# Loading later head pairs one stage earlier, holding one pair's loads for VectorE, and a changed order of stages, in windowed attention followed by a gated FFN

## The chip, the cores and the metric

The kernel runs on 1 core of one Trainium2 chip. The metric is the device time in microseconds (us); smaller is better. The trace's own span is some 1.8 us shorter than that time, so spans are compared with spans and times with times. Ratios are of fast runs alone; medians and ranges are of all runs of a kernel, a few slow ones among them. One trace, named below, is of a slow run and is not compared. The record also has the mean granted TensorE clock of every run: 0.998 or more, or 0.994 or less, and nothing between. Traces at 1.000 show no stretch of half clock, those from 0.981 to 0.994 one or two.

## The reference, cut to what matters

```python
# batch 4, 8 heads, 768 positions, head size 64; 4 sink positions, window of 128
scores = scale * q @ k^T;  keep = is_sink | (0 <= row - col < 128)
a = softmax(where(keep, scores, -1e9));  attn = a @ v           # (4, 8, 768, 64)
x = attn, heads side by side: (3072, 512)
out = (relu(x @ w_gate) * (x @ w_val)) @ w_out                  # d_ff = 1536
```

## The kernel before

Two heads make a pair; pairs are numbered 0 to 15, four to a batch. A pair's attention is cut into stages: three score groups (`s(0..2)`), the second half of the pair before it (`v`), preparing the next pair and loading later ones (`t`), and the first half of its own normalization (`v0`). A plan weaves these stages between the chunks of the FFN, which keeps TensorE filled. All engines follow one program order; waits come from data and buffers.

```python
def unit_stages(x):
    u, prev, nxt = U[x], at(x - 1), at(x + 1)
    def s(gi):
        def f():
            ...                                   # (cut)
            if gi == 0 and nxt is not None and nxt.xbar:   # pairs 8 to 15
                nxt.X()                           # DMA transposes of keys, queries (SyncE)
            u.S(gi)                               # scores, exponential, mask
        return f
    def v():  ...  norm(prev, 1)                  # (cut)
    def t():
        if nxt is not None:
            if not nxt.xbar:
                nxt.T(not on_array)               # pairs 1 to 7: transposes on TensorE
            nxt.sinkk()                           # VectorE: sink keys, needs nxt's kT
        if x == 3:   load(6)
        elif x == 4: load(7)
        elif x >= 5: held(x + 3)
        if 4 <= x < 6:
            for c in ((0,), (1, 2))[x - 4]: load_wo(c)
        if at(x + 3) is not None:
            casts(at(x + 3), "kqv")               # GpSimd: float32 to bf16
            ...                                   # (cut)
        if x in (0, 1, 3, 4): load_w((0, 1, 1, 2, 3)[x])
        if x == 0:   load(5)
    ...

def held(x):                                      # the loads wait for VectorE
    if x < len(U):
        nc.vector.memset(U[x].stg[0:1, 0:1], 0.0)
        load(x)

PLAN = ((0, 28), (24, 50), (48, 62), (71, 74))    # (chunk, stages done by then)
```

`load` puts keys, queries and two value halves of a pair (1.18 MB) in SyncE's DMA queue. `load_w` and `load_wo` put weights in GpSimd's. A staging buffer serves every fourth pair.

The softmax here doesn't subtract the row's maximum and nothing guards it: scores larger than these inputs give would overflow.

Of the kernel before, what the change touches and what calls it, by code (L numbers as in the profile page):

```python
# [33 lines left out]
def kernel(  # L34
# [179 lines left out]
    def warm(n):  # L214

        if not warm_ps:
            warm_ps.append(ps_gv.tile([128, 512], F32, name="warm", tag="gv"))
        for _ in range(n):
            nc.tensor.matmul(out=warm_ps[0][:, 0:128], lhsT=ident[:], rhs=ident[:], start=True, stop=True,
                             skip_group_check=True)  # L220

    def load_w(c):
        n = d_ff // 4
        for w, dst in ((moe_w_gate, wg), (moe_w_val, wv)):
            nc.gpsimd.dma_start(out=dst[:, :, c * n:(c + 1) * n],  # L225
                                in_=w.rearrange("(ko ki) n -> ki ko n", ki=128)[:, :, c * n:(c + 1) * n])

    def load_wo(c):
        nc.gpsimd.dma_start(out=wo[:, 4 * c:4 * c + 4, :],
                            in_=moe_w_out.rearrange("(ko ki) n -> ki ko n", ki=128)[:, 4 * c:4 * c + 4, :])  # L230


    def setup_pool():
        make_identity(nc, ident)
        t0, a = bias[:, 0:255], bias[:, 503:754]
        for x, w, d in ((t0, 255, 0), (a, 251, 4)):
            nc.gpsimd.memset(x, 0.0)
            nc.gpsimd.affine_select(out=x, in_=x, compare_op=Alu.is_ge, fill=NEG, base=d,
                                    pattern=[[1, w]], channel_multiplier=-1)
            nc.gpsimd.affine_select(out=x, in_=x, compare_op=Alu.is_ge, fill=NEG, base=127 - d,  # L240
                                    pattern=[[-1, w]], channel_multiplier=1)

    def setup_slot(s):
        nc.vector.memset(kT[s][:, S:872], 0.0)

    def setup_m0():

        cp, ms = nc.gpsimd.tensor_copy, nc.gpsimd.memset
        ms(bias[0:4, 0:128], 0.0)
        ms(bias[0:4, 128:255], NEG)  # L250
        cp(bias[:, 255:503], bias[:, 503:751])
        ms(bias[0:4, 255:503], 0.0)
        ms(bias[0:4, 503:627], NEG)
# [64 lines left out]
    with tc.manual_schedule():  # L318
        U = [Unit(i) for i in range(B * NP)]
        on_array = []  # L320

        def at(x):
            return U[x] if 0 <= x < len(U) else None

        def casts(u, what, eng=nc.gpsimd):
            for w in what:
                u.cast(w, eng)

        def load_t(b):

            nc.sync.dma_start(out=vt[b % 2][:], in_=v[b, :, 744:768, :].rearrange("h s d -> s h d"))  # L331

        def cast_t(b):
            nc.gpsimd.tensor_copy(v6[b % 2][0:24, :, :], vt[b % 2][:])

        def load(x):
            if not U[x].p:
                load_t(U[x].b)
            for f in (lambda e: U[x].load_kq("k", e), lambda e: U[x].load_kq("q", e),
                      lambda e: U[x].load_v(e, 0), lambda e: U[x].load_v(e, 1)):  # L340
                f(nc.sync)

        def held(x):
# [5 lines that stand above are left out]
        for y in ("k0", "q0", "k1", "q1", "v1", "t", "k2", "q2", "v2", "k3", "q3", "v3"):  # L349
            if y == "t":  # L350
                load_t(0)
            elif y[0] in "kq":
                U[int(y[1])].load_kq(y[0], nc.sync)
            else:
                for h in (0, 1) if y[0] == "v" else ("ab".index(y[0]),):
                    U[int(y[1])].load_v(nc.sync, h)
        nc.vector.memset(ones[:], 1.0)
        setup_pool()
        setup_m0()
        nc.scalar.activation(ee[0][:, 0, 0, 0:64], ones[:], Act.Exp, bias=0.0, scale=1.0)  # L360
        for h in range(2):
            U[0].load_v(nc.scalar, h)
        for x in range(2):
            nc.vector.memset(v6[x][:], 0.0)
        setup_slot(0)
        setup_slot(1)
        warm(36)
        casts(U[0], "k", nc.vector)
        casts(U[0], "q", nc.scalar)
        casts(U[1], "kq")  # L370
        casts(U[0], "v")
        cast_t(0)
        casts(U[1], "v")
        casts(U[2], "kqv")
        load(4)


        stages = []
# [6 lines that stand above are left out]
                    if gi == 0 and u.p == 0:  # L385
                        xTs[u.b] = xpool.tile([128, NP, S], BF16, name="xT")
                    if gi == 0 and nxt is not None and nxt.xbar:
                        nxt.X()
                    u.S(gi)
                    if x == 0 and gi < 2:  # L390
                        warm(5)
                return f

            def v():
                if prev is not None:
                    norm(prev, 1, ps_at if on_array else ps_gv)
# [4 lines that stand above are left out]
                        nxt.T(not on_array)  # L401
                    nxt.sinkk()
                if x == 3:
                    load(6)
                elif x == 4:
                    load(7)
                elif x >= 5:
                    held(x + 3)
                if 4 <= x < 6:
                    for c in ((0,), (1, 2))[x - 4]:  # L410
                        load_wo(c)
                if at(x + 3) is not None:
                    casts(at(x + 3), "kqv")
                    if (x + 3) % NP == 0:
                        cast_t((x + 3) // NP)
                if x in (0, 1, 3, 4):
                    load_w((0, 1, 1, 2, 3)[x])
                if x == 0:
                    load(5)
            def v0():  # L420
                norm(u, 0, ps_at if on_array else ps_gv)

            def both(f, g):
                return lambda: (f(), g())
            if x < NP:
                return [s(0), v, s(1), t, s(2), v0]
            return [both(v, s(0)), both(t, s(1)), both(v0, s(2))] if x >= 8 else [s(0), v, s(1), t, s(2), v0]

        def first():
            U[0].T(True)  # L430
            U[0].sinkk()
            setup_m1()
        stages.append(first)
        for x in range(len(U)):
            stages += unit_stages(x)
        stages.append(lambda: norm(U[-1], 1))

        si = 0
        f2 = deque()
        total = len(stages)  # L440

        ORDER = [(0, h, m) for g in range(0, FM, 3) for h in range(2) for m in range(g, g + 3)]
        ORDER += [(b, h, m) for b in range(1, B) for h in range(2) for m in range(FM)]
        PLAN = ((0, 28), (24, 50), (48, 62), (71, 74))

        def want(ci):
            for (c0, w0), (c1, w1) in zip(PLAN, PLAN[1:]):
                if ci <= c1:
                    return w0 + (w1 - w0) * (ci - c0) // (c1 - c0)
            return total  # L450
        count = {}
        n = S // 2
        for ci, (b, h, m) in enumerate(ORDER):
            if b not in hTs:
                hTs[b] = hpool.tile([128, FM, S], BF16, name="hT", tag="hT")
            while si < min(total, want(ci)):
                stages[si]()
                si += 1
            if not ci:
                on_array.append(1)  # L460
            chunk(b, h * n, n, m)
            for _ in range(min(3, len(f2))):
                f2.popleft()()
            count[b, h] = count.get((b, h), 0) + 1
            if count[b, h] == FM:
                for t in range(3 * h, 3 * h + 3):
                    w = d_model // 2 if (b, t) == (B - 1, 5) else d_model
                    for c in range(0, d_model, w):
                        for mm in range(FM):
                            f2.append(lambda b=b, t=t, mm=mm, c=c, w=w: ffn2(b, t, mm, b == B - 1, c, w))  # L470
        while f2:
            f2.popleft()()
# [33 lines left out]
```

## Time and profile before

| | |
|---|---|
| time, median of the first 3 runs | 260.46 us (259.57 to 260.71) |
| span of the profiled run | 258.7 us, TensorE busy 249.4 us |
| TensorE's waits in the middle of the run | 2.0 us for `hT` at 74 us, 1.1 us for `wv` at 30 us |
| granted TensorE clock | 1.00 |

In the lines of waits, the columns are who waited, the source line, for whom, the us in total, the number of waits and the longest. In the timelines they are start, duration, engine, line, operation and tiles; the bracket gives the idle time just before and what ended it. `kT<-kn` is a DMA transpose of keys; `stg` are staging buffers.

### The profile page before, as it was taken

The numbers are of one execution on the slowest core, as the hardware profiler recorded it, in microseconds if no ns is written. First come the engines' busy times: TensorE is split into PE (matmuls) and PEld (weight loads), VectorE is DVE, ScalarE is ACT, GpSimd is POOL, SyncE is SP. The second block draws the span as 40 slices with busy tenths as digits, with TensorE's granted clock in tenths as the row PEclk, the third lists the DMA queues.
The fourth block names the chain that finished last, engine by engine and source line by source line (L and its number), as shares of the span: only waits on it lengthen the run. The fifth ranks groups of instructions, "written<-read, shape, count | busy, mean of one in ns | idle before, by whom it ended". The sixth has DMA issues, their size and how long they took to land.

```text
span 258.7 us, 5201 instructions
## 1 busy us (share of the span) xinstructions
PE 249.4 (96%) x2046; PEld 143.5 (55%) x2046; DVE 144.5 (56%) x313; ACT 115.6 (45%) x188; POOL 62.3 (24%) x94
## 2 busy tenths in 40 slices
PE   7999799999969999999999999999999999999994
PEld 7565466565545555546555555556555555555443
DVE  2598869886748564756656665756664322322100
ACT  3887665647424444443535344344533332333212
POOL 6779538801535221404040210000000000000000
PEclk9999999999999999999999999999999999999999
DMA  7999999999989948869491961311011101111132
GB/s 213 309 279 253 246 257 197 196 198 199 218 125 239 197 111 157 129 145 138 85 242 43 184 104 42 61 43 41 3 41 41 42 1 41 43 41 41 41 112 94
DMA packets 77320, 33.56 MB, mean 130 GB/s; under 512 B 64368, under 2 KB 74352, under 8 KB 77296
## 3 DMA queue, kind: packets, MB, share of 16 engines
q1 hardware_dynamic: 69920, 28.12, 48.5%
q0 software_dynamic: 5808, 4.72, 12.1%
q10 hardware_dynamic: 1568, 0.39, 0.7%
q8 instruction: 16, 0.26, 0.5%
q14 instruction: 8, 0.07, 0.1%
HBM read 28.51 MB, written 6.29 MB: 135 GB/s over the span
## 4 chain that ended last, share of the span: by engine, by line
PE 68%; DMA 13%; SPq 8%; POOL 6%; issue 2%; DVE 1%; ACT 0%; POOLq 0%; DVEq 0%; ACTq 0%
PE op L310 23%; PE gp L290 19%; PE vp L296 18%; DMA stg<-in_v_dram 11%; PE ops L206 5%; SPq L119 4%; PE sps L181 3%; SPq L114 2%; DMA kT<-kn 2%; POOL vn L129 2%; SPq L111 1%; SPq L331 1%; POOL kn L126 1%; POOL vn L130 1%; POOL wg L225 1%
## 5 line engine op out<-in xcount | busy, mean ns | idle before, releaser
L298 DVE TENSOR_TENSOR hT<-gs,vp 128x384 bf16<-128x384 f32 x96 | 52.8, 550 | 54.4 <-PE vp L296 52.7
L290 PE MATMUL gp<-xT,wg 128*128 128x384 bf16 x384 | 78.5, 327 | 2.0 <-DVE hT L298 2.0
L296 PE MATMUL vp<-xT,wv 128*128 128x384 bf16 x384 | 78.1, 326 | 1.1 <-DMA wv<-in_moe_w_val_dram 1.1
L293 ACT ACTIVATE gs<-gp 128x384 f32<-128x384 f32 x96 | 47.1, 490 | 61.5 <-PE gp L290 60.3
L310 PE MATMUL op<-wo,hT 128*128 128x512 bf16 (+1 forms) x300 | 74.4, 370 | 0.0
L185 ACT ACTIVATE ee<-sps 128x1006 bf16<-128x1006 f32 (+2 forms) x48 | 46.1, 966 | 46.9 <-PE sps L181 46.8
L296 PEld LDWEIGHTS <-wv 128*128 128x128 bf16 x384 | 37.5, 98 | 26.2 <-DMA wv<-in_moe_w_val_dram 1.5
L290 PEld LDWEIGHTS <-wg 128*128 128x128 bf16 x384 | 34.0, 98 | 31.8 <-issue 6.7
L310 PEld LDWEIGHTS <-hT 128*128 128x128 bf16 x300 | 29.4, 98 | 25.0
L187 DVE TENSOR_TENSOR ee<-ee,msk 128x1006 bf16<-128x1006 bf16 (+2 forms) x36 | 25.1, 698 | 11.3 <-ACT ee L185 11.3
L126 POOL CAST kn<-stg 128x768 bf16<-128x768 f32 x15 | 13.2, 879 | 59.0 <-DMA stg<-in_k_dram 39.6
L314 ACT COPY ot<-op 128x512 f32<-128x512 f32 (+1 forms) x25 | 14.2, 569 | 24.5 <-PE op L310 24.5
L275 DVE STREAM_TRANSPOSE R<-ops 128x384 f32<-128x384 f32 x24 | 13.9, 581 | 12.6 <-PE ops L206 12.5
L278 DVE STREAM_TRANSPOSE R<-rc 128x384 f32<-128x384 f32 x32 | 18.5, 578 | 1.1
L280 DVE TENSOR_TENSOR xT<-ops,R 128x384 bf16<-128x384 f32 x32 | 17.8, 557 | 1.7
L206 PEld LDWEIGHTS <-ones 128*64 128x64 bf16 x288 | 12.3, 109 | 11.2 <-issue 10.8
L129 POOL CAST vn<-stg 128x768 bf16<-128x768 f32 x16 | 13.3, 832 | 15.0 <-DMA stg<-in_v_dram 15.0
L126 POOL CAST qn<-stg 128x768 bf16<-128x768 f32 x15 | 13.3, 888 | 11.9 <-DMA stg<-in_q_dram 7.1
L206 PE MATMUL ops<-ee,vn 128*64 128x255 bf16 (+7 forms) x256 | 15.3, 240 | 0.2 <-DVE xT L280 0.2
L181 PE MATMUL sps<-qT,kT 64*128 64x251 bf16 (+2 forms) x128 | 14.7, 252 | 0.5 <-ACT qT L154 0.4
L181 PEld LDWEIGHTS <-kT 64*128 64x128 bf16 x128 | 6.3, 93 | 12.9 <-issue 10.5
L181 PE MATMUL sps<-qT,kTs 64*128 64x248 bf16 (+1 forms) x96 | 12.3, 253 | 0.0
(57 smaller groups left out, 135.5 us busy)
## 6 DMA issues: line engine op xcount, KB each, us to landing
stg<-in_k_dram SPq DMA_DIRECT2D x16, 384.0 KB, 4.9
stg<-in_q_dram SPq DMA_DIRECT2D x16, 384.0 KB, 5.4
out_dram<-ot SPq DMA_DIRECT2D x23, 256.0 KB, 2.0
stg<-in_v_dram SPq DMA_DIRECT2D x30, 192.0 KB, 5.4
wg<-in_moe_w_gate_dram POOLq DMA_DIRECT2D x4, 384.0 KB, 7.7
wv<-in_moe_w_val_dram POOLq DMA_DIRECT2D x4, 384.0 KB, 9.8
wo<-in_moe_w_out_dram POOLq DMA_DIRECT2D x3, 512.0 KB, 13.6
stg<-in_v_dram ACTq DMA_DIRECT2D x2, 192.0 KB, 6.4
```

The costliest lines, as they stand in the source:

```text
L126: cp((self.kn if what == "k" else self.qn)[:], self.staging(what).rearrange("p h (n d) -> p n h d", d=64))
L129: eng.tensor_copy(self.vn[:], self.staging("v"))
L181: nc.tensor.matmul(out=ps[:, h, c:c + w], lhsT=self.kw(j, r), rhs=qT[s][r, qa:qa + w], start=not self.biased, stop=True, skip_group_check= ...
L185: nc.scalar.activation(x, ps[:, :, 0:c], Act.Exp, bias=0.0, scale=scale)
L187: nc.vector.tensor_tensor(x, x, bc(msk[:, m0:m0 + c], 2), op=Alu.mult)
L206: nc.tensor.matmul(out=ps[1 - what][64 * h:64 * h + 64, qa - q0:qa - q0 + w], lhsT=self.vw(j, h) if what else ones[:], rhs=ee[s][:, gi, h, ...
L278: nc.vector.transpose(r[:, 1, 0:w], bass.AP(a.tensor, a.offset, [a.ap[0], [1, nb], [0, 32]]))
L290: nc.tensor.matmul(out=gp[:, 0:n], lhsT=wg[:, ko, m * 128:(m + 1) * 128], rhs=x[:, ko, c0:c0 + n], start=ko == 0, stop=ko == KO - 1)
L293: nc.scalar.activation(gs[:, 0:n], gp[:, 0:n], Act.Relu, bias=0.0, scale=1.0)
L296: nc.tensor.matmul(out=vp[:, 0:n], lhsT=wv[:, ko, m * 128:(m + 1) * 128], rhs=x[:, ko, c0:c0 + n], start=ko == 0, stop=ko == KO - 1)
L298: nc.vector.tensor_tensor(hT[:, m, c0:c0 + n], gs[:, 0:n], vp[:, 0:n], op=Alu.mult)
L310: nc.tensor.matmul(out=op, lhsT=hTs[b][:, m, t * 128:(t + 1) * 128], rhs=wo[:, m, c0:c0 + n], start=m == 0, stop=m == FM - 1)
```

## The change

The intent is to give the first weights the DMA engines to themselves (pair 5, which stood beside them, now waits for VectorE), to load pairs 8 to 15 one stage earlier, and to let scores run ahead of the previous pair's normalization.

```diff
                 if x == 3:
+                    held(5)
+                    casts(U[5], "kqv")
                     load(6)
                 elif x == 4:
                     load(7)
-                elif x >= 5:
-                    held(x + 3)
+                if x >= 4:
+                    held(x + 4)
 ...
-                if at(x + 3) is not None:
+                if at(x + 3) is not None and x != 2:
+                    pass
                     casts(at(x + 3), "kqv")
 ...
-                if x == 0:
-                    load(5)
 ...
             if x < NP:
-                return [s(0), v, s(1), t, s(2), v0]
+                return [s(0), s(1), v, t, s(2), v0]
 ...
-        PLAN = ((0, 28), (24, 50), (48, 62), (71, 74))
+        PLAN = ((0, 28), (6, 32), (24, 50), (48, 62), (71, 74))
```

## The prediction

> **What bounds the kernel now.** I name a pair of heads by its index 0 to 15 (batch 0 is pairs 0 to 3); the title's "sixth pair" is pair 5. I read the page's busy times first, then who TensorE waited for, then the chain of waits, then the timelines of SyncE, GpSimd and VectorE around each wait, then the DMA queues stretch by stretch. First the page (busy us, share, instructions):
>
> ```profile
> PE 249.4 (96%) x2046; PEld 143.5 (55%) x2046; DVE 144.5 (56%) x313; ACT 115.6 (45%) x188; POOL 62.3 (24%) x94
> ```
>
> Then TensorE's own waits (who waited for whom: us in total, times, longest):
>
> ```profile
> PE gp L290 <- DVE hT L298: 2.0, 1, 2.0
> ...
> PE vp L296 <- DMA wv<-in_moe_w_val_dram: 1.1, 1, 1.1
> ...
> PE sps L181 <- ACT qT L154: 0.4, 1, 0.4
> ```
>
> TensorE is the bound: 249.4 of 258.7 us. The other 9.3 us are 2.0 us at the start, 3.3 us at the tail (240 us on: busy 15.4 of 18.7), and three waits that an order of loads could touch: 1.1 us for the first value weights at 30 us, 0.4 us at 27 us, and 2.0 us near 74 us. Everything the change could win is therefore 3.5 us, or 1.3%. What it could lose is not limited so.
>
> The 2.0 us wait says "hT", but the VectorE timeline names its cause: VectorE sat 4.93 us at pair 8's sink keys, which come by a DMA transpose. Next, lines of the timelines of SyncE, VectorE and TensorE that lead there (start, duration, in brackets the idle time before):
>
> ```profile
> 47.18 0.37 SPq L111 DMA_DIRECT2D stg<-in_k_dram  x1
> ...
> 51.01 12.26 SPq L119 DMA_DIRECT2D stg<-in_v_dram  x2
> 63.35 2.67 SPq L111 DMA_DIRECT2D stg<-in_k_dram  x1
> ...
> 69.84 1.62 SPq L135 DMA_TRANSPOSE kT<-kn  x1
> ...
> 74.87 0.41 DVE L161 COPY kTs<-kT 128x372 bf16<-128x372 bf16 x1 [4.93 <-DMA kT<-kn]
> ...
> 75.87 0.81 PE L290 MATMUL gp<-xT,wg 128*128 128x384 bf16 x4 [1.97 <-DVE hT L298]
> ```
>
> Pair 8's loads are issued from 47.18, pair 9's from 63.35, and only then pair 8's transposes at 69.84. SyncE's queue is in program order, so pair 8's transposes stand behind pair 9's bytes; the last value cast of pair 9 starts at 74.31, when its data has landed, and the transpose lands at 74.84. TensorE resumes 1.0 us later, at 75.87, and from there to the end has no wait worth naming. So **the time is 75.87 us plus 182.8 us**, and it moves one for one with that landing as long as TensorE is there waiting for it.
>
> The DMA queues between 53 and 63.5 us show why pair 8 needs 20 us from issue to landing:
>
> ```profile
> q0 software_dynamic: 1804, 1.57, 91.1%
> q1 hardware_dynamic: 1788, 0.45, 32.7%
> ```
>
> Equal numbers of packets go from the weight queue (q0) and from SyncE's (q1), but a weight packet carries 768 bytes or more, a row of pair 8 only 256. So q1 gets a quarter of the bytes, 0.043 MB/us, and the sum is 0.19 MB/us. From 45.5 to 66 us the same view gives 3.00 + 1.09 MB, 0.20 MB/us with all DMA engines busy.
>
> **What the Trainium skill says.** "DMA: Bandwidth & Descriptors", section "Queues, rings and completion order": each DMA engine takes turns between its queues packet by packet, and consumes one queue's descriptors in ring order. The trace agrees with both: 1804 against 1788 packets, and the transpose landing just behind pair 9. The same page's section "Issuing engines are not separate DMA queues": transfers from different issuers share the same 16 engines. Holding pair 5 back thus does give the weights its bandwidth, but only moves the bytes. "TensorE: Matmul & The Clock Gate", opening table, calls VectorE's queue a strict FIFO; the 4.93 us in which VectorE did none of the ready FFN products agrees.
>
> **The change part by part.**
>
> (a) Scores of the second group before the previous pair's normalization, pairs 0 to 3. The same instructions move; nothing is added. TensorE is busy 9.75 of 10 us between 10 and 20 us and 9.4 in the next 10, so all there is to win is the 0.4 us for `qT` at 27 us: ScalarE's idle gaps of 0.7 to 0.8 us before the second exponential go and its copies end earlier. Against it, two score banks must be released sooner. I give it 0.3 us.
>
> (b) Pair 5 waits for VectorE. Its loads, issued from 19.39 before, now follow a 59 ns memset of VectorE behind pair 4's sink keys. Those end at 27.0 now; with (a) I put it at 26.5, so the loads are issued from 26.6. The first weights (issued 21.25, landing about 28 and 31 now) should land near 28 both, as pair 4's bytes are nearly through by 22 us: the wait of 1.1 us goes. But the second weights are issued at 26.3 and pair 5 now meets those instead. Keys and queries are 0.79 MB (2 x 384 KB). In 30 to 36 us q1 shared with weights and moved 0.94 MB, 0.157 MB/us: 5.0 us. From 26.6, with about 1.4 us to the first byte (76.7 for an issue at 75.40), they land near 33 to 34.5; the query cast takes 0.83 us and the transposes on TensorE 0.33 us after it. TensorE arrives for these transposes at about 31.8 (33.03 before less the 1.1 us), has them at 35 to 36.5 against an end of 33.70 before. **The wait of 1.1 us is exchanged for one of 3 to 4 us**; net 1.3 to 2.8 us later at this point.
>
> (c) Pairs 8 on are loaded one stage earlier (the held load of pair x+4, not x+3, at stage t of pair x). This reads as a gain: pair 8 is released near 38 us, not 47. But the transposes of pair 8 stay where they were, at the first stage of pair 7, and stage t of pair 6 comes before that. Before, that stage issued pair 9; now it issues pair 10. So **pair 8's transposes now stand behind pair 10 too**: 1.18 MB more (k, q, two v). The windows 67 to 72 us show 1.17 MB of such rows in 5.0 us, so 5.0 us. What comes off: between 42.5 and 45 us the engines moved only 59 GB/s (pair 7 done, third weights not started), about 0.35 MB below the 0.20 MB/us that they do later. Pair 8 is now queued there and fills a part. But pair 5, held, makes pairs 6 and 7 end about 1 us later, so I count 0.25 MB, 1.2 us. Sum: the transposes land 3.8 us later, at about 78.7 rather than 74.84. What was a stall of 4.9 us for VectorE becomes one of 6 to 8.
>
> (d) The new plan point (6, 32) runs 4 stages in the first 6 chunks where 5.5 ran, and returns to the old plan at chunk 24. Nothing is added; stage t of pair 4 stays at chunk 2 and that of pair 7 at chunk 21. I count 0.
>
> The sum: (a) and (b) leave TensorE 1 to 2.8 us late on the way to 74 us, but there it stood waiting for 2.0 us and now the target is 3.8 us later, so these are absorbed. What remains is (c): 260.46 + 3.8 = **264.3 us**, 1.5% longer.
>
> **Rivals.**
>
> First: the earlier loads free the transpose (the evident intent). If pair 8's transposes land by 73 us, the 2.0 us go, and with (b) at its cheapest the time is about 259.5 us. For it: pair 8 can be released 9 us earlier. Against it: the DMA engines are full from 46 to 72 us in the page's row, so an earlier release only joins the same line, and SyncE's program order puts pair 10 ahead of the transposes. I see no way to over 2% faster: it needs 5.2 us and all waits that the change touches are 3.5.
>
> Second: TensorE's wait in (b) decides instead. If pair 5 is starved by the weights as pair 8 was (3.7 us passed between its issue at 47.18 and its bytes), its queries land at 37 and the shift at chunk 2 is 4 to 5 us. Then the end is again 263.5 to 265 us. Both lie on the same path, so the later one counts, not the sum.
>
> Third: the bytes in front of the transposes cost more. At 0.19 MB/us (the rate next to weights) pair 10 costs 6.2 us, with no credit for the gap: 266.7 us, over the 2% line at 265.7.
>
> **Range and chances.** From rival one at its best, with a little lost, to rival three and a little: 261.3 to 267.3 us. Faster by over 2%: 0.01. Slower by over 2% needs the transposes 5.2 us later, which is between my estimate and rival three: 0.24. Within 2%: 0.75.
>
> **What will show it.** (b): TensorE waits for GpSimd's cast of `qn` or `kn` at 32 to 36 us, and the wait for `wv` is gone. (c): in SyncE's timeline the loads of three pairs stand between 40 us and the first transpose, and VectorE waits 6 us or more for `kT<-kn`, to land at 77 to 80. The wait of TensorE for `hT` near 74 to 80 us is then 2 to 5 us. After it nothing differs: the rest takes 182.8 us, within 1 us. I am wrong if that transpose lands before 74.8, if it is issued before pair 10's loads, or if a new wait appears after 80 us because later transposes, too, stand behind one pair more.

## The result, and the profile after

The changed kernel takes 268.38 us (median of 4 runs, 266.89 to 268.88); the kernel before, run beside it, 260.58 us (259.57 to 261.67). The ratio is 1.0289, 95% interval 1.0229 to 1.0349: slower, and above the predicted range of 261.3 to 267.3. A ratio is the mean time of one kernel's fast runs over that of the other's of the same rounds, so it is not quite the ratio of the medians.

Busy time and TensorE's clock by slice, from the page of the changed kernel:

```profile
PE 252.4 (95%) x2023; PEld 145.0 (54%) x2046; DVE 143.9 (54%) x314; ACT 116.1 (44%) x188; POOL 61.3 (23%) x94
...
PEclk9999967999997999999999999999999999999999
```

The clock row is new: all nines before, and now two dips, in slices 6 and 7 (33 to 47 us) and in slice 13 (80 to 87 us). The matmuls are the same (23 of their records are missing from the later trace), and TensorE is busy 3.0 us longer. TensorE's waits in the changed kernel:

```profile
PE tkq L149 <- POOL kn L126: 2.7, 1, 2.7
PE gp L290 <- DVE hT L298: 2.4, 1, 2.4
PE tkq L149 <- POOL qn L126: 1.6, 1, 1.6
```

The wait of 1.1 us for `wv` is gone, and 4.3 us for pair 5's casts stand in its place. The wait for `hT` is still there, 7 us later. Lines of the timelines that lead to it:

```profile
71.38 0.53 SPq L111 DMA_DIRECT2D stg<-in_k_dram  x1
...
76.42 1.62 SPq L135 DMA_TRANSPOSE kT<-kn  x1
...
81.72 0.41 DVE L161 COPY kTs<-kT 128x372 bf16<-128x372 bf16 x1 [5.23 <-DMA kT<-kn]
...
82.73 0.81 PE L290 MATMUL gp<-xT,wg 128*128 128x384 bf16 x4 [2.40 <-DVE hT L298]
```

The load at 71.38 is pair 10's; pair 8's transposes come after it. TensorE resumes at 82.73, against 75.87 before: 6.9 us of the 8.3 us by which the span grew. From there to the end it takes 184.3 us against 182.8, the other 1.4 us. Two stretches, with columns stretch, length, busy time of TensorE, its weight loads, VectorE, ScalarE and GpSimd, granted clock, DMA share and GB/s, show what that is:

```profile
37.00:42.00 5.00, 4.94 (x24) 2.55 (x25) 1.01 (x5) 2.76 (x4) 2.01 (x4) 0.50 1.02 281
...
84.00:86.00 2.00, 2.00 (x11) 0.68 (x11) 1.90 (x5) 0.06 (x1) 0.05 (x1) 0.50 1.29 261
```

After each of the two waits TensorE's granted clock is 0.50 for some us. The first FFN product after pair 5's transposes, a group of four matmuls, in the changed kernel and in the kernel before:

```profile
37.67 1.49 PE L290 MATMUL gp<-xT,wg 128*128 128x384 bf16 x4
```

```profile
33.70 0.81 PE L290 MATMUL gp<-xT,wg 128*128 128x384 bf16 x4
```

TensorE is busy, and it goes at half pace: the next group starts 1.28 us later here (38.95), 0.65 us later there (34.35).

### The profile page after: what moved, and what is told of

Its sections match the earlier page's. It is cut to its first block, busy times and chain, and to the rows that moved or that the text cites. A ratio compares the mean times of both kernels' runs of the same rounds, so it can differ in the third digit from the quotient of the medians.

```text
span 267.0 us, 5185 instructions
## 1 busy us (share of the span) xinstructions
PE 252.4 (95%) x2023; PEld 145.0 (54%) x2046; DVE 143.9 (54%) x314; ACT 116.1 (44%) x188; POOL 61.3 (23%) x94
## 4 chain that ended last, share of the span: by engine, by line
PE 82%; DMA 7%; DVE 6%; issue 1%; ACT 1%; POOL 1%; SPq 0%; DVEq 0%; ACTq 0%; POOLq 0%
PE gp L290 25%; PE op L310 23%; PE vp L296 23%; PE ops L206 7%; DMA stg<-in_q_dram 5%; PE sps L181 4%; DMA kT<-kn 2%; DVE R L278 1%; DVE R L275 1%; DVE kTs L161 1%; DVE xT L280 1%; PE tkq L149 1%; DVE rc L276 1%; ACT ee L185 0%; PE sps L176 0%
## 5 line engine op out<-in xcount | busy, mean ns | idle before, releaser
L290 PE MATMUL gp<-xT,wg 128*128 128x384 bf16 x384 | 79.8, 331 | 2.9 <-DVE hT L298 2.4
L296 PE MATMUL vp<-xT,wv 128*128 128x384 bf16 x384 | 79.4, 330 | 0.4 <-DVE R L275 0.3
L310 PE MATMUL op<-wo,hT 128*128 128x512 bf16 (+1 forms) x277 | 71.3, 373 | 1.2
L129 POOL CAST vn<-stg 128x768 bf16<-128x768 f32 x16 | 14.0, 873 | 31.3 <-DMA stg<-in_v_dram 15.6
L126 POOL CAST qn<-stg 128x768 bf16<-128x768 f32 x15 | 12.4, 830 | 12.1 <-DMA stg<-in_q_dram 7.4
L161 DVE COPY kTs<-kT 128x372 bf16<-128x372 bf16 x16 | 6.6, 415 | 15.9 <-ACT kT L154 10.6
```

The costliest lines, as they stand in the source:

```text
L126: cp((self.kn if what == "k" else self.qn)[:], self.staging(what).rearrange("p h (n d) -> p n h d", d=64))
L290: nc.tensor.matmul(out=gp[:, 0:n], lhsT=wg[:, ko, m * 128:(m + 1) * 128], rhs=x[:, ko, c0:c0 + n], start=ko == 0, stop=ko == KO - 1)
L296: nc.tensor.matmul(out=vp[:, 0:n], lhsT=wv[:, ko, m * 128:(m + 1) * 128], rhs=x[:, ko, c0:c0 + n], start=ko == 0, stop=ko == KO - 1)
L310: nc.tensor.matmul(out=op, lhsT=hTs[b][:, m, t * 128:(t + 1) * 128], rhs=wo[:, m, c0:c0 + n], start=m == 0, stop=m == FM - 1)
```

## The experiments

The theory after the result: two waits on one path. Pair 5's hold makes TensorE late (its wait, then half clock). Pair 10's place ahead of pair 8's transposes makes those land late. The later of the two at about 80 us sets the end, and half clock comes on top. Rivals: the order of stages costs; the hold is all of it; the place of the transposes is all of it; the clock is no cost of its own.

### The order alone (e1_order)

```diff
-                return [s(0), v, s(1), t, s(2), v0]
+                return [s(0), s(1), v, t, s(2), v0]
-        PLAN = ((0, 28), (24, 50), ...
+        PLAN = ((0, 28), (6, 32), (24, 50), ...
```

> The kernel before with only the two changes of order: second score group ahead of the previous normalization for pairs 0 to 3, and the new plan point. Theory (the loss lies in the two changes of loads): within 0.8 us of before, 259.7 to 261.3; TensorE's 0.4 us wait for qT near 27 us gone, the wait near 74 us again about 2 us. Rival (the order itself costs): over 263 us.

Measured: 261.12 us against 260.48, ratio 1.0032 (1.0007 to 1.0057). Who TensorE waited for:

```profile
PE sps L181 <- DVE kTs L162: 1.6, 4, 0.6
...
PE gp L290 <- DVE hT L298: 1.0, 1, 1.0
```

The wait for `qT` went as foretold; the wait near 74 us is 1.0 us where about 2 was expected. Four short waits for the sink keys, 1.6 us in all, came between 13 and 29 us: the reordered scores ask for them sooner. They don't set the end of the traced run: TensorE still waits for pair 8's keys afterwards and resumes at 76.09, against 75.87. What the 0.3% is made of is not shown; 12 of these 20 runs had a stretch of half clock (mean clock 0.994 or less), 8 of the 23 of the kernel before. So the order wins nothing, and it is not the loss.

### The hold of pair 5 alone (e2_hold5)

```diff
                 if x == 3:
+                    held(5)
+                    casts(U[5], "kqv")
                     load(6)
-                if at(x + 3) is not None:
+                if at(x + 3) is not None and x != 2:
-                if x == 0:
-                    load(5)
```

> The kernel before with only pair 5's loads held for VectorE (and its casts moved). Theory: two effects on one path. TensorE waits about 4.3 us for the casts of pair 5 and runs at half clock for some us after, and the 1.1 us wait for wv goes: TensorE is 5 to 6.5 us late at 74 us. Pair 8's transpose, with only pair 9 ahead of it, lands about 2 to 3 us later than the 74.84 of before, so TensorE waits for it hardly any more. Time 264 to 265.5 us. If the transposes alone set the time (rival), it is 262 to 263.5.

Measured: 264.32 us, ratio 1.0156 (1.0093 to 1.0219), inside the theory's range and outside the rival's. TensorE's waits, then VectorE's arrival at the transposed keys of pair 8:

```profile
PE tkq L149 <- POOL kn L126: 2.3, 1, 2.3
PE tkq L149 <- POOL qn L126: 1.8, 1, 1.8
```

```profile
75.92 0.43 DVE L161 COPY kTs<-kT 128x372 bf16<-128x372 bf16 x1 [0.31 <-DMA kT<-kn]
```

TensorE lost 4.1 us here, the granted clock was 0.72 on average from 37 to 43 us, and the keys landed near 75.9, 1 us later than before (the expectation had 2 to 3). VectorE waited only 0.3 us for them and TensorE not at all: with the hold alone, TensorE's lateness is the loss.

### The earlier loads alone (e3_early)

```diff
-                elif x >= 5:
-                    held(x + 3)
+                if x >= 4:
+                    held(x + 4)
```

> The kernel before with only the held loads one stage earlier (pair x+4 at stage t of pair x), so that pair 10 stands ahead of pair 8's transposes. Theory: no wait near 32 us beyond the 1.1 us for wv; the transpose lands 3.5 to 5.5 us later than 74.84, at 78.3 to 80.3; TensorE waits 5.5 to 7.5 us there and then runs some us at half clock, 1 to 2 us more. Time 265 to 267.5 us. Rival (the earlier loads are harmless, the held pair 5 is all of the loss): 258.5 to 261.

Measured: 267.2 us, ratio 1.0255 (1.0204 to 1.0307). The lines where VectorE and TensorE go on:

```profile
79.11 0.37 DVE L161 COPY kTs<-kT 128x372 bf16<-128x372 bf16 x1 [6.49 <-DMA kT<-kn]
```

```profile
80.07 1.44 PE L290 MATMUL gp<-xT,wg 128*128 128x384 bf16 x4 [3.47 <-DVE hT L298]
```

The keys land at 79.1 us, 4.2 us later than before, in the fastest of the four runs (266.04 us); TensorE waits 3.5 us where the expectation had 5.5 to 7.5. In this run it had itself come later: it waited 1.9 us for `wv`, ran at 0.66 clock from 32 to 37 us, and took 1.46 us for a group of four matmuls that took 0.81. From 80 to 84 the clock was 0.60 on average. The verdict does not rest on that: the loads, meant as a help, cost 6.7 us by themselves.

### The changed kernel with the transposes first (e4_xfirst)

```diff
-                if x >= 4:
+                if 4 <= x < 6:
                     held(x + 4)
 ...
                     if gi == 0 and nxt is not None and nxt.xbar:
                         nxt.X()
+                        held(x + 3)
```

> The changed kernel, but from pair 10 on the held loads are issued just behind the transposes of the stage, not ahead of them, so that only pair 9 stands ahead of pair 8's transposes. Theory: the transpose lands 5 us earlier than in the changed kernel, at 76 to 77.5; TensorE arrives there at 80 us (late from pair 5's wait and half clock) and no longer waits: 4 to 5 us... of the 2.4 us wait and the 1.5 us of half clock that follows it are gone, 264 to 265.5 us. If the transposes' place alone makes the loss (rival), it is 260 to 262; if their place does not matter, 267.5 to 269.

Measured: 264.19 us, ratio 1.0151 (1.0084 to 1.0218). SyncE issues the transposes earlier than in the changed kernel's 76.42, and no wait for `kT` is left in VectorE's list or for `hT` in TensorE's:

```profile
72.25 1.31 SPq L135 DMA_TRANSPOSE kT<-kn  x1
```

Only pair 5's wait is left, and the time equals that of the hold alone. The four corners, each a median of all its runs:

| | pair 10 behind pair 8's transposes | pair 10 ahead of them |
|---|---|---|
| pair 5 early | 260.5 (before), 260.65 (e6_best) | 267.2 (e3_early) |
| pair 5 held | 264.3 (e2_hold5), 264.2 (e4_xfirst) | 268.4 (the change) |

Each fault alone costs 4 to 7 us, both together 8, not 10.5: they lie on one path and the later one counts.

### Idle matmuls in the wait, on both variants (e5_keep_xfirst, e5b_keep)

```diff
+            if self.i == 5:
+                kp = ...                          # (cut) a PSUM tile that nothing reads
-            for x, p_, n in ((self.kn, ps, 5), (self.qn, pq, 7)):
+            for x, p_, n in ((self.kn, ps, 24), (self.qn, pq, 30)):
+                for _ in range(n if self.i == 5 else 0):
+                    nc.tensor.matmul(out=kp[:, 0:128], lhsT=ident[:], rhs=ident[:], start=True, stop=True, ...)
 ...
```

> The kernel with the transposes first (e4_xfirst), with 54 idle matmuls of 128 columns (about 3.5 us at full clock) put into TensorE's wait for pair 5's casts, so that its clock should not fall. They are in a wait, so they cost nothing there. Theory (half clock after the wait is a part of the loss of its own, about 2.5 us between 37 and 43 us): granted clock 1.0 from 37 to 43 us, time 2 to 2.6 us below the 264.2 of e4_xfirst, 261.5 to 262.3. Rival (the clock is not a cost of its own): 263.5 to 265.

Measured: 261.61 us (261.11 lowest), ratio to before 1.0039 (1.0018 to 1.0061), so 2.6 us below e4_xfirst's 264.19. These two ran in different calls; their ratios to the kernel before, 1.0151 and 1.0039, say the same. The profiled run fell in the slow state (266.76 us), so its trace is not compared. The clock of the fast runs is on record all the same: 0.998 to 1.000 in all 19 of them, against 0.987 to 0.993 in the four of e4_xfirst.

> The changed kernel with the same idle matmuls in the wait for pair 5. Here the transposes of pair 8 land last (81.7 us), whenever TensorE arrives. Theory (the landing sets the end): TensorE arrives 2.5 us earlier, waits 4.5 to 5 us instead of 2.4, and the time stays within 1 us of the changed kernel, 267.4 to 269.4. Rival (TensorE's lateness after the wait for pair 5 sets the end): 2 to 2.6 us faster, 265.5 to 266.5.

Measured: 267.89 us, ratio 1.0255 (1.021 to 1.03). Its stretch from 37 to 43 us, and the lines where VectorE and TensorE go on at the transposed keys:

```profile
37.00:43.00 6.00, 6.00 (x64) 3.91 (x62) 3.13 (x8) 3.52 (x6) 3.29 (x5) 1.00 1.14 316
```

```profile
80.44 0.40 DVE L166 COPY kTs<-kT 128x372 bf16<-128x372 bf16 x1 [6.14 <-DMA kT<-kn]
```

```profile
81.44 0.81 PE L295 MATMUL gp<-xT,wg 128*128 128x384 bf16 x4 [3.48 <-DVE hT L303]
```

The clock stayed at 1.00, TensorE came to the keys at 77.96 (81.44 less 3.48) instead of 80.33 (82.73 less 2.40), 2.4 us earlier. It waited 1.1 us longer there, not 2.4, since in this run the keys landed 1.3 us earlier, too. The same 54 matmuls win 2.6 us where TensorE is late and 0.5 us (by the two ratios 0.9, and the ranges of the two kernels overlap) where the transposes are: half clock is a cost of its own, and in the changed kernel the landing of pair 8's keys is the end of the path.

### Can both be had? (e6_best, e7_best_w0)

```diff
 # e6_best, against the kernel before
-                elif x >= 5:
-                    held(x + 3)
+                if 4 <= x < 6:
+                    held(x + 4)
 ...
                         nxt.X()
+                        held(x + 3)
 # e7_best_w0 besides
+                    casts(at(x + 3), "kq")
+                    if x == 0: load_w(0)
+                    casts(at(x + 3), "v")
```

> The kernel before, pair 5 loaded early as before, pairs 8 and 9 loaded one stage earlier as in the change, from pair 10 on loads just behind the stage's transposes. Theory: pair 8 fills the gap of the DMA engines between 42.5 and 45 us; its transpose has only pair 9 ahead and lands at 73 to 74.5 instead of 74.84; the wait for hT near 74 us shrinks from 2.0 to under 1.5 us; the wait for wv stays. Time 258.5 to 260.3 against 260.5. If the earlier loads harm by themselves (by taking bandwidth from the weights), 261 or more.

Measured: 260.65 us against 260.84, ratio 0.9995 (0.9972 to 1.0018): the same. What VectorE and TensorE waited for, and TensorE's clock afterwards:

```profile
72.61 0.33 DVE L161 COPY kTs<-kT 128x372 bf16<-128x372 bf16 x1 [0.20 <-DMA kT<-kn]
```

```profile
32.06 1.25 PE L296 MATMUL vp<-xT,wv 128*128 128x384 bf16 x4 [1.72 <-DMA wv<-in_moe_w_val_dram]
```

```profile
32.00:34.00 2.00, 1.94 (x7) 0.97 (x8) 1.25 (x3) 0.00 (x0) 0.00 (x0) 0.58 1.20 257
```

The keys land at 72.6 us, 2.2 us earlier than before, and the wait at 74 us is gone, as expected. The gain went into the wait for `wv`: 1.7 us in this run, with 0.58 clock behind it.

> e6_best with the first weights issued by GpSimd 1.4 us earlier, ahead of pair 3's value cast. Theory: they land by 30 us, the 1.1 us wait for wv goes: 1 us below e6_best if the transposes of pair 8 have landed by then, else within 0.5 us of e6_best, because that landing and not TensorE's arrival is then the end of the path: 257.5 to 260.

Measured: 260.44 us, ratio 0.9997 (0.9972 to 1.0022): a miss. The weights were issued at 19.9 us instead of 21.4, and the wait for `wv` was still 1.9 us. A likely reason, not tested: issued earlier, they met the keys and queries of pair 5 for longer. Their queue moved 0.27 MB from 19.5 to 25 us (0.01 in e6_best), but only 0.52 MB from 25 to 32 us (0.85), while SyncE's moved 1.38 MB (0.63).

### Values of pair 5 late, and idle matmuls at the first weights (e8_v5_late, e9_keep_wv)

```diff
 # e8_v5_late, against e6_best: keys and queries of pair 5 early as before, values held
                 if x == 3:
+                    nc.vector.memset(U[5].stg[0:1, 1536:1537], 0.0)
+                    for h in range(2): U[5].load_v(nc.sync, h)
+                    casts(U[5], "v")
                     load(6)
 ...                                       # (cut) keys and queries loaded and cast where pair 5 was before
 # e9_keep_wv, against e6_best
+        if (b, c0, m) == (0, 0, 0):
+            for _ in range(24):
+                nc.tensor.matmul(out=gp[:, 384:512], lhsT=ident[:], rhs=ident[:], ...)
```

> e6_best, in which the wait for the first value weights was 1.7 us and TensorE then ran at 0.57 clock from 32 to 36 us. Here only the values of pair 5 (256-byte rows, not needed before 48 us) wait for VectorE; its keys and queries stay early. Theory (what the hold was for can be had without the wait that it made): the weights have the engines from 25 us on and land by 29.5 us, no wait for wv, clock 1.0 from 32 to 36 us, no wait for pair 5's casts over 0.5 us. TensorE comes to 72 us 2.5 to 3.5 us earlier and may wait up to 1.5 us there for pair 8: 257 to 259 us against 260.6 of e6_best. If it waits for pair 5 or pair 8 instead, 260 or more.

Measured: 260.11 us (22 runs, 258.35 to 262.44) against 260.79, ratio 0.9974 (0.9951 to 0.9996). In the trace the wait for `wv` is gone and so is the dip of the clock, without a wait for pair 5. The first value product starts here:

```profile
30.57 0.81 PE L296 MATMUL vp<-xT,wv 128*128 128x384 bf16 x4 [0.27 <-DVE R L275]
```

The profiled run took 258.68 us, as expected; the median did not. It is the only version with an interval below 1, by a quarter of a per cent.

> e6_best with 24 idle matmuls of 128 columns in the wait for the first value weights, nothing else. Theory (half clock after that wait is a cost of its own): clock 1.0 from 32 to 36 us, 1.5 to 2.2 us below e6_best, 258.4 to 259.3. Rival: within 0.5 us of e6_best.

Measured: 259.98 us, ratio 0.9976 (0.9945 to 1.0008). The clock was 1.00 from 32 to 36 us, and the profiled run 259.3 against 261.0 of e6_best's, but the medians differ by 0.7 us only, under the expected 1.5. Single executions of the kernel before range from 258.6 to 264.0 us, so a wait and a dip of the clock seen in one trace need not be in every run.

How often the dip comes is in the clocks on record. Of the 117 runs of the kernel before that stood beside e1 to e9, 35 had a stretch of half clock, with a mean time of 262.1 us against 260.2 for the other 82 (13 of the 35 are among those called slow). So had 10 of 22 runs of e6_best, 6 of 22 of e7_best_w0, 3 of 22 of e8_v5_late and 1 of 14 of e9_keep_wv. Among runs without it, the mean of e8_v5_late is 259.8 us and that of e9_keep_wv 260.0, against 260.3 of the kernel before in the same call. So the gain from e6_best's trace, which has the dip, to e9_keep_wv's, which has not, is larger than that of the medians: the dip was in fewer than half of e6_best's runs.

## Why the prediction was wrong

**What bounds the kernel, and which path moves the time: right.** The end moved with the landing of pair 8's keys, and TensorE's lateness in between was absorbed. e5b_keep shows it: TensorE 2.4 us earlier at the keys, 0.5 us less time. Where pair 10 is not in front (e2_hold5, 264.3 us), the second rival came true: TensorE's lateness sets the end.

**(a) and (d), the order: small as said, wrong in sign.** 0.3 us of gain was forecast; e1_order lost 0.3%, and what that is made of stays open.

**(b), TensorE's wait for pair 5: right in kind, too small.** Forecast 3 to 4 us, measured 2.71 + 1.63 = 4.3 us. The net lateness was forecast at 1.3 to 2.8 us and is 4.0 (37.67 against 33.70), since pair 5's queries landed near 36.1 us and not by 34.5. (The 1.4 us to the first byte is misread: bytes move from 76.4 us on for the issue at 75.40.) What followed was not in the working: half clock from 37 to about 43 us, 2.4 us more. TensorE came to the keys 6.4 us later than before (80.33 against 73.90).

**(c), pair 10 ahead of the transposes: right in mechanism.** Its loads stand in front, and e4_xfirst, which puts them behind, takes 4.2 us less. The first rival, a freed transpose, needed what e4_xfirst and e6_best change. Of the signs named, VectorE's wait came out at 5.2 us and not at 6 or more, since VectorE, too, came later (76.49 against 69.94).

**The step that failed is the sum of (c): "the transposes land 3.8 us later".** They landed 6.9 us later (81.72 against 74.87). Its terms, as predicted and as the traces have them:

| term | predicted | measured |
|---|---|---|
| pair 10 in front | 5.0 us later | 6.5 (79.11 of e3_early against 72.61 of e6_best, with the same early release) |
| pairs 8 and 9 released earlier | 1.75 us sooner (0.35 MB) | 2.3 (72.61 against 74.87) |
| pair 5 held | 0.5 us later (0.10 MB off that credit) | 2.6 (81.72 against 79.11) |

The third rival's 6.2 us for pair 10 was nearer. How the miss of 3.1 us divides between pair 10 and the hold is not settled, since each landing is of one run, and e3_early's trace is of its fastest. By the medians the early loads alone cost 6.7 us, some 1.4 of it the clock after the wait, so 5.3 where the first two terms make 3.25; and the hold adds 1.2 us to them (0.9 by the two ratios). Other traces give the hold 1.0 us (e2_hold5, 75.92, against the kernel before) and 1.3 us (e5b_keep, 80.44, against e3_early). The order of stages, which differs here too, moved the landing by 0.3 us alone (75.21 in e1_order). So both were counted too small: the early loads by 1.0 us in the traces and 2.0 us by the medians, the hold, at 0.9 to 2.6 us, by at least 0.4.

For the hold the prediction had quoted that it "only moves the bytes", and then charged half a microsecond for it ("so I count 0.25 MB", in place of 0.35). The DMA queues between 21.5 and 30 us, first in the kernel before, then in the changed one (packets, MB, share):

```profile
q0 software_dynamic: 1045, 0.78, 63.7%
q1 hardware_dynamic: 2312, 1.23, 54.5%
```

```profile
q0 software_dynamic: 1176, 0.88, 83.9%
q1 hardware_dynamic: 1079, 0.38, 18.6%
```

The weights got 0.10 MB more; SyncE's queue moved 0.85 MB less. In sum 0.75 MB was not moved while the engines were there for it, 3.7 us at the 0.20 MB/us that they do when full. The bytes held back had to be moved later, ahead of pair 8's, and a part was won back. The same queues from 21.5 to 72 us, in e3_early, which has the same early loads, and in the changed kernel:

```profile
q1 hardware_dynamic: 17888, 6.47, 59.8%
q0 software_dynamic: 5808, 4.72, 59.2%
```

```profile
q0 software_dynamic: 5808, 4.72, 61.7%
q1 hardware_dynamic: 15847, 5.95, 53.3%
```

At 72 us SyncE's queue is still 0.52 MB behind, 2.6 us at that rate. In e5b_keep it is 0.42 MB behind, and the keys land 1.3 us later than in e3_early, so the bytes don't give the landing to the microsecond. One more part was not tested: in the changed kernel SyncE stood 0.8 us (53.5 to 54.3) until VectorE, late with TensorE, released pair 9; in e5b_keep it did not.

**The second term that was missing is the clock.** "After it nothing differs: the rest takes 182.8 us, within 1 us" was wrong, as the rest took 184.3 us: the clock fell after the second wait, too. The Trainium skill's "TensorE: Matmul & The Clock Gate", section "Part 1: The HAM clock gate", says that TensorE drops to half its clock after an idle window of about 3.4 us. The prediction cited that page for VectorE's queue and did not ask what a longer wait does to the clock. The trace agrees with the half (0.50), but the second wait, at 2.40 us, is shorter than that window (see the end). Together, 3.1 us of later landing and 1.4 us of clock make 4.5 us, the difference between the predicted span (264.3 less 1.8, so 262.5) and the measured 267.0.

## What to carry to other kernels

Before a load is issued earlier, look at what stands behind it in the same queue: here the loads meant to help went ahead of the transposes that the next stage was waiting for, and putting them behind these took 4.2 us off the changed kernel. A load that is held so that another can pass leaves its bytes to be moved later, and if the engines are full until the next deadline, that deadline moves. When a change lengthens a wait of TensorE from 1 or 2 us to 3 or 4, count the slow matmuls after it as well. Look for them in the clock of every run, not in one trace alone: the kernel before, with waits of 1 to 2 us and none in its trace, had them in 35 of 117 runs.

## What the Trainium skill lacked or had wrong

- "TensorE: Matmul & The Clock Gate", Part 1 and section "Why this matters for your kernels" (one idle window of about 3.4 us, no gaps over about 3 us): here shorter single waits were followed by half clock, 1.72 us (e6_best at 32 us) and 2.40 us (the change at 82.7 us), and 1.97 us (the kernel before at 75.9 us) was not. Nor does the share of the last 3.4 us in which TensorE was busy tell them apart: 1.44 us in e6_best, where the clock fell, and 1.43 us in the kernel before, where it did not. One program, the kernel before, fell to half clock in 35 of 117 runs and not in the others. The page calls the window free-running, which would fit if a partly idle window is enough; no run here shows its phase.
- The same page tells no worth of idle matmuls put into a wait that can't be removed: 54 of 128 columns in a wait of 4 us were worth 2.6 us here (e5_keep_xfirst against e4_xfirst), where that wait was the end of the path.
- "DMA: Bandwidth & Descriptors", section "Queues, rings and completion order", says that engines take turns between queues by packets, but not what that does to two queues of unlike packets: 1804 against 1788 packets in 10.5 us gave 1.57 MB to one and 0.45 MB to the other.
